# Attention and expert layers on one core: a planner's durations, the token ranks, the first denominators and the first loads are changed

## The chip, the core and the metric

The kernel runs on one core of a Trainium2 chip. The metric is the device time of one execution in microseconds (us). Engines are named as the profile names them: PE (TensorE) multiplies, DVE (VectorE) and ACT (ScalarE) do the element-wise work, POOL (GpSimd) casts and issues indirect DMAs, SP (SyncE) issues the other DMAs.

## What is computed

The reference has two parts. Attention over 8 batches, 12 heads, 448 tokens and 64 columns per head, with capped scores:

```
scores = cap * tanh(scale * (q @ k.T) / cap)        # cap = 30
attn   = exp(scores - max) / (sum + 1e-9)
x      = attn @ v                                   # heads side by side: 768 columns
```

and, batch by batch, one expert for the 128 tokens that score highest:

```
score   = x @ w_gate                                # 448 scores
top     = 128 tokens with the highest score
y       = relu(x[top] @ w1) @ w2                    # 768 -> 1024 -> 768
out     = x;  out[top] += sigmoid(score[top]) * y
```

## The kernel before, in words

**Doubles.** Four heads form a *double*: two row groups and two column groups of PE, 64 by 64 each, so that four matmuls (a *quartet*) run side by side. There are 24 doubles, three for each batch. A double has seven steps of 64 keys. A step is a quartet of scores on PE (L297, into `ps`), a tanh over 128x896 on ACT (L337), an exponential in place (L340, tile `p`), a quartet of products with v (L305, accumulated in `acc`), and on DVE an addition of the exponentials into `e` (L350, six per double). After the last step one quartet with a matrix of ones sums `e` over the keys (L384, `sums`), DVE transposes products (L376) and sums (L392), takes reciprocals (L398, L400), normalises (L425), and multiplies by the gate vector and reduces (L447, L451).

**Selection.** When a batch's three doubles are done, DVE adds the partial scores (L472, L474), PE folds them (L478) so that each token has its own partition, DVE copies them (L484), PE spreads them along a row (L489), DVE copies the row (L494) and counts for each token how many score higher (L502) and how many equal ones stand before it (L510), four pieces of 128 tokens each, adds the two counts (L517) and compares them with 0 to 127 (L553). PE multiplies that matrix with the token numbers and scores (L558), and POOL gathers the 128 rows from memory (L569).

**Expert.** The gathered rows and both weight matrices are split in a high and a low part, and three products of parts are summed, all in full 128x128 matmuls (L635): 36 of 512 columns for w1 and 48 of 384 for w2 in each batch. The text calls them *heavy*. The weights arrive in 14 pieces, through three staging buffers: SP loads a piece (L253), POOL casts it to the high part (L256), DVE subtracts to get the low part (L259).

**Order.** Every instruction of the fast path belongs to a task with an engine, an estimated duration, a priority, and buffers that it takes and gives back. `Plan.run` plays these tasks through by the estimates, before the kernel is built, and writes each engine's instructions in the order in which it started them. Engines work strictly in that order. `SEEN` is what the planner adds until another engine sees a result. On PE, `pick_pe` decides between attention (mode "att") and full-array work (mode "full"): it visits heavy work for `VISIT` = 2000 ns at a time, and while attention is left it stops heavy work when only `RESERVE` = 42000 ns of it remain. The reserve covers the last batch's selection.

Of the kernel before, what the change touches and what calls it, by code (L numbers as in the profile page):

```python
# [22 lines left out]
EPS = 1e-9  # L23
WARM = 3
# [3 lines left out]
SEEN = {"NONE": 0, "PE": 240, "ACT": 90, "DVE": 90, "POOL": 120, "SP": 0}  # L28
# [3 lines left out]
RESERVE = 42000  # L32


class Task:

    def __init__(self, eng, ns, fn, deps=(), prio=0.0, take=(), give=(), lat=0, mode=None,
                 heavy=False):
        self.eng, self.ns, self.fn, self.prio, self.lat = eng, ns, fn, prio, lat
        self.take, self.give, self.mode, self.heavy = take, give, mode, heavy  # L40
        self.after = []
# [7 lines left out]
class Plan:  # L49
# [28 lines left out]
    def run(self, after_attention):  # L78
# [4 lines left out]
        self.att_left = sum(t.mode == "att" for t in self.tasks)  # L83
        self.heavy_left = sum(t.ns for t in self.tasks if t.heavy)
# [4 lines left out]
        while started < len(self.tasks):  # L89
            for e in SEEN:  # L90
# [7 lines left out]
                if e == "PE":  # L98
# [4 lines left out]
                    if t.mode == "att":  # L103
                        self.att_left -= 1
                        if not self.att_left:
                            after_attention()
# [41 lines left out]
    def pick_pe(self):  # L148
# [22 lines left out]
def load_flag(tc, K, cap):  # L171
    nc = tc.nc
    cp = K.const
    K.cap = cp.tile([P, 1], F32, name="capc")
    nc.sync.dma_start(K.cap, cap.to_broadcast([P, 1]))
# [19 lines left out]
    K.rk = [cp.tile([P, K.NCH], F32, name=f"rk{i}") for i in range(2)]  # L195
    K.before = cp.tile([P, K.NCH * P], BF16, name="before")
    K.fold = cp.tile([P, 4, Q], F32, name="fold")
    K.ones = cp.tile([P, HD], F32, name="ones")
    K.hs = cp.tile([P, 1024], F32, name="hs")
    K.room = cp.tile([P, 6 * K.S], F32, name="room")  # L200
    K.used = 0

    def early(n):
        K.used += n
        return K.room[:, K.used - n:K.used]

    K.early = early


def load_consts(tc, K):  # L210
# [6 lines left out]
    for vt, sc, rk, far in zip(K.vals, K.score, K.rk, (1e6, 0.0)):  # L217
# [3 lines left out]
        nc.vector.memset(rk, far)  # L221
    nc.vector.tensor_reduce(K.fold[:, 0, :], K.ident.rearrange("p (a i) -> p i a", i=Q),
                            axis=AX.X, op=ALU.add)
    for g in range(1, 4):
        nc.vector.tensor_copy(K.fold[:, g, :], K.fold[:, 0, :])
    nc.gpsimd.memset(K.before, 1.0)
    nc.gpsimd.affine_select(K.before, K.before, pattern=[[-1, K.NCH * P]],
                            compare_op=ALU.is_gt, fill=0.0, base=(K.NCH - 1) * P,
# [85 lines left out]
def attention_tasks(tc, K, D):  # L314
# [13 lines left out]
    for s in range(NS):  # L328
# [18 lines left out]
        def sum2(t, s=s):  # L347
            if s == 1:
                D.E = w_tile(K, [P, 2, S], F32, "E", t.got["E"], "e")
# [558 lines left out]
```

## Time and profile before

| | |
|---|---|
| runs before | 496.62, 497.96, 499.25 us (median 497.96) |
| the profiled execution | 497.39 us, of which the profile's span is 495.7 us |
| first quartet, first heavy matmul, last four heavy matmuls begin | 6.60, 93.01, 488.52 us after the span's start |
| PE busy | 463.2 us (93% of the span) |
| DVE busy | 399.9 us (81%) |
| ACT busy | 346.8 us (70%) |
| POOL busy | 43.0 us (9%) |

The profile has one execution. A timeline row gives the start, the time from the first start to the last end, the engine, the instructions and, in brackets, how long the engine had been idle and what released it. Durations of neighbours overlap a little, so what an instruction costs its engine's queue is the distance between starts. A step's quartet on PE is eight records, since the profile shows each of the four float32 matmuls as two.

### The profile page before, as it was taken

The numbers are of one execution on the slowest core, as the hardware profiler recorded it, in microseconds if no ns is written. First come the engines' busy times: TensorE is split into PE (matmuls) and PEld (weight loads), VectorE is DVE, ScalarE is ACT, GpSimd is POOL, SyncE is SP. The second block draws the span as 40 slices with busy tenths as digits, with TensorE's granted clock in tenths as the row PEclk, the third lists the DMA queues.
The fourth block names the chain that finished last, engine by engine and source line by source line (L and its number), as shares of the span: only waits on it lengthen the run. The fifth ranks groups of instructions, "written<-read, shape, count | busy, mean of one in ns | idle before, by whom it ended". The sixth has DMA issues, their size and how long they took to land.

```text
span 495.7 us, 9354 instructions
## 1 busy us (share of the span) xinstructions
PE 463.2 (93%) x3750; PEld 243.3 (49%) x3750; DVE 399.9 (81%) x671; ACT 346.8 (70%) x394; POOL 43.0 (9%) x40
## 2 busy tenths in 40 slices
PE   5968999899999999999999999999999999859994
PEld 2222233443654465445554655455554533239984
DVE  1699999999989878988789679987789699987311
ACT  4957998679576986877777777977767799810210
POOL 1331121110020001100020000100020001000000
PEclk9988999999999999999999999999999999989998
DMA  6825864356141631553333532534323641032101
GB/s 212 337 85 177 204 191 132 113 141 173 56 153 47 180 96 39 176 128 96 112 103 105 158 75 74 176 95 130 112 70 119 176 112 34 0 75 70 33 32 38
DMA packets 50660, 57.42 MB, mean 116 GB/s; under 512 B 17968, under 2 KB 44720, under 8 KB 50608
## 3 DMA queue, kind: packets, MB, share of 16 engines
q1 hardware_dynamic: 49328, 50.44, 36.0%
q0 software_dynamic: 1280, 6.29, 3.8%
q8 instruction: 32, 0.52, 0.5%
q14 instruction: 20, 0.16, 0.1%
HBM read 42.57 MB, written 14.16 MB: 114 GB/s over the span
## 4 chain that ended last, share of the span: by engine, by line
PE 65%; DVE 19%; issue 5%; DMA 4%; ACT 4%; POOLq 0%; POOL 0%; DVEq 0%
PE pb L635 25%; PE acc L305 18%; PE ps L297 16%; DVE e L350 7%; PE sums L384 4%; ACT p L337 2%; PE pb L598 1%; DVE jk L447 1%; DMA xe<-out,idx 1%; DMA stage<-in_moe_w 1%; DVE part L451 1%; DVE sm L392 1%; ACT p L340 1%; DVE jk L502 1%; DMA q<-in_q 1%
## 5 line engine op out<-in xcount | busy, mean ns | idle before, releaser
L337 ACT ACTIVATE p<-ps,sc 128x896 f32<-128x896 f32 x168 | 165.0, 1007 | 84.7 <-PE ps L297 81.8
L340 ACT ACTIVATE p<-p,capc 128x896 f32<-128x896 f32 x168 | 170.4, 1046 | 2.0
L305 PE MATMUL acc<-p,v 64*64 64x448 f32 x1288 | 147.5, 552 | 2.0 <-ACT p L340 1.6
L297 PE MATMUL ps<-q,k 64*64 64x448 f32 x1288 | 145.4, 542 | 3.1 <-ACT p L337 1.8
L350 DVE TENSOR_TENSOR e<-e,p 128x896 f32<-128x896 f32 x120 | 132.1, 1101 | 20.0 <-ACT p L340 15.6
L297 PEld LDWEIGHTS ps<-q,k 64*64 64x64 f32 x1288 | 47.3, 133 | 80.5 <-issue 34.6
L305 PEld LDWEIGHTS acc<-p,v 64*64 64x64 f32 x1288 | 44.6, 134 | 71.8 <-issue 46.6
L569 POOL DMA_INDIRECT xe<-out,idx x8 | 13.1, 1634 | 297.8 <-DVE gt L575 297.8
L384 PE MATMUL sums<-e,ones 64*64 64x448 f32 x192 | 24.3, 577 | 12.1 <-DVE e L350 11.9
L376 DVE STREAM_TRANSPOSE xT<-acc 128x896 f32<-128x896 f32 x24 | 26.6, 1110 | 9.4 <-PE acc L305 9.3
L656 ACT ACTIVATE hs<-pb 128x512 f32<-128x512 f32 x16 | 9.5, 598 | 35.3 <-PE pb L635 34.6
L635 PE MATMUL pb<-w2l,hh 128*128 128x384 f32 x128 | 30.6, 349 | 0.0
L392 DVE STREAM_TRANSPOSE sm<-sums 128x896 f32<-128x896 f32 x24 | 26.6, 1107 | 4.8 <-PE sums L384 4.7
L350 DVE TENSOR_TENSOR e<-p 128x896 f32<-128x896 f32 x24 | 26.0, 1083 | 5.4 <-ACT p L340 5.4
L635 PE MATMUL pb<-w2h,hl 128*128 128x384 f32 x128 | 29.8, 346 | 0.0
L635 PE MATMUL pb<-w2h,hh 128*128 128x384 f32 x128 | 29.1, 350 | 0.5 <-DVE hl L605 0.5
L635 PE MATMUL pb<-w1h,xh 128*128 128x512 f32 x96 | 27.6, 409 | 0.0
L635 PE MATMUL pb<-w1h,xl 128*128 128x512 f32 x96 | 27.2, 405 | 0.0
L451 DVE TENSOR_REDUCE part<-jk 128x14 f32<-128x896 f32 x24 | 26.1, 1086 | 0.8
L635 PE MATMUL pb<-w1l,xh 128*128 128x512 f32 x96 | 26.1, 400 | 0.0
L635 PEld LDWEIGHTS pb<-w2h,hh 128*128 128x128 f32 x128 | 22.9, 192 | 5.1 <-issue 2.4
L635 PEld LDWEIGHTS pb<-w2h,hl 128*128 128x128 f32 x128 | 22.4, 189 | 2.8 <-issue 2.8
(82 smaller groups left out, 392.6 us busy)
## 6 DMA issues: line engine op xcount, KB each, us to landing
q<-in_q SPq DMA_DIRECT2D x46, 224.0 KB, 3.9
k<-in_k SPq DMA_DIRECT2D x46, 224.0 KB, 3.8
v<-in_v SPq DMA_DIRECT2D x23, 448.0 KB, 4.2
out<-xn SPq DMA_DIRECT2D x16, 224.0 KB, 4.4
out<-room SPq DMA_DIRECT2D x16, 224.0 KB, 3.7
stage<-in_moe_w SPq DMA_DIRECT2D x6, 384.0 KB, 3.0
stage<-in_moe_w SPq DMA_DIRECT2D x4, 512.0 KB, 6.9
out<-xn SPq DMA_DIRECT2D x16, 112.0 KB, 2.4
```

The source lines that it names most:

```text
L297: tc.nc.tensor.matmul(K.ps[HALF[r], j, :K.S], lhsT=D.k[r][HALF[j], ks], rhs=D.q[r][HALF[j], :], start=True, stop=True)
L305: tc.nc.tensor.matmul(D.acc[HALF[j], r, :K.S], lhsT=D.v[HALF[r], s, j, :], rhs=D.P[s][HALF[r], j, :], start=(s == 0), stop=(s == K.NS - 1))
L337: nc.scalar.activation(D.P[s], box["ps"][:, :, :S], AF.Tanh, scale=K.sc)
L340: nc.scalar.activation(D.P[s], D.P[s], AF.Exp, scale=K.cap)
L350: nc.vector.tensor_tensor(D.E, D.P[0] if s == 1 else D.E, D.P[s], op=ALU.add)
L376: nc.vector.transpose(D.xT, D.acc[:, :, :S])
L384: nc.tensor.matmul(D.sums[HALF[j], r, :S], lhsT=K.ones[HALF[r], :], rhs=D.E[HALF[r], j, :], start=True, stop=True)
L392: nc.vector.transpose(D.sm, D.sums[:, :, :S])
L451: nc.vector.tensor_reduce(K.part[b][:, grp, :], jk, axis=AX.X, op=ALU.add)
L569: nc.gpsimd.indirect_dma_start(out=X["xe"][:M], out_offset=None, in_=K.out[:(b + 1) * S, :], in_offset=bass.IndirectOffsetOnAxis(ap=X["idx ...
L635: nc.tensor.matmul(X["acc" + n_ops][:M, :ns[1]], lhsT=X[l][:, i, :M], rhs=K.wts[r][:, i, ns[2]], start=bool(start and n == 0), stop=(stop ...
L656: nc.scalar.activation(K.hs[:M, fs], X["acc" + nm][:M], AF.Relu)
```

## The change

- **Durations.** The planner's estimates become shorter: tanh and exponential 905 and 935 ns in place of 1030 and 1075, and others likewise; `SEEN` for ACT and DVE rises from 90 to 170.
- **Last sums.** The last double's sums are marked `late`; once only they are left of attention, heavy work is allowed below the reserve.
- **Ranks.** One operation for 128 tokens does both counts: it subtracts the token's own score from the row and compares with a table that holds a tiny positive number for the token itself and later ones, and zero for earlier ones (L536). The rank matrix is one operation (L569), the sum of two counts is gone, the fold is four matmuls of 32 columns so that two copies are enough (L513, L517, L520).
- **First two doubles.** DVE adds only the first five exponentials. The last two are summed on PE, by a quartet each, on top of the quartet for `e` (`sum_groups`, L416).
- **Loads.** The first q, k and v are issued before anything else, half of q and k and the cap on ACT's queue; the first three weight pieces are issued before the third double's q and k.

```
-SEEN = {..., "ACT": 90, "DVE": 90, ...}
+SEEN = {..., "ACT": 170, "DVE": 170, ...}
+EARLY = 2
...
-        if self.att_left and self.heavy_left <= RESERVE:
+        if self.main_left and self.heavy_left <= RESERVE:
             heavy = []
-        if self.mode == "att" and att:
+        if att and (self.mode == "att" or not self.main_left):
             return first(att)
...
+    tc.nc.scalar.dma_start(K.cap, cap.to_broadcast([P, 1]))
+    first.load_qk(tc, K, 0, None)
+    first.load_qk(tc, K, 1, None, tc.nc.scalar)
+    first.load_v(tc, K, None)
...
-        a = K.plan.add("SP", 600, load, prio=6 + 3 * n, ...)
+        a = K.plan.add("SP", 600, load, prio=6 + 3 * n if n > 2 else n - 4, ...)
-        l = K.plan.add("DVE", 1250, low, ...)
+        l = K.plan.add("DVE", 240 + 0.9 * m, low, ...)
...
+def sum_groups(d, n):
+    if d < EARLY:
+        return [list(range(n - 2)), [n - 2], [n - 1]]
+    return [list(range(n))]
...
-        th = add("ACT", 1030, tanh, ...)
-        ex_ = add("ACT", 1075, exp, ...)
+        th = add("ACT", 905, tanh, ...)
+        ex_ = add("ACT", 935, exp, ...)
...
+        for n, part in enumerate(parts):
             for r in range(2):
                 for j in range(2):
+                    nc.tensor.matmul(D.sums[HALF[j], r, :S], lhsT=K.ones[HALF[r], :],
+                                     rhs=part()[HALF[r], j, :], start=(n == 0),
+                                     stop=(n == len(parts) - 1))
+    su = add("PE", 752 * len(parts), sums, ready, ..., late=D.d == K.B * K.NG - 1)
...
-        nc.vector.tensor_scalar(jk[:m], box["row"][:m], score[:m, c:c + 1], None, op0=ALU.is_gt,
-                                op1=ALU.add, accum_out=rk[0][:m, c:c + 1])
...
+        nc.vector.scalar_tensor_tensor(out=jk[:m], in0=box["row"][:m], scalar=score[:m, c:c + 1],
+                                       in1=K.least[:m, at:at + S], op0=ALU.subtract,
+                                       op1=ALU.is_ge, accum_out=K.rk[:m, c:c + 1])
...
+        nc.vector.scalar_tensor_tensor(
+            out=X["sel"], in0=K.iota.unsqueeze(1).to_broadcast([P, NCH, P]), scalar=float(s0),
+            in1=K.rk.unsqueeze(2).to_broadcast([P, NCH, P]), op0=ALU.add, op1=ALU.is_equal)
```

What the planner makes of it, at three places. First DVE at the end of the first double (`w1l` is the low part of a weight piece, `stage` and `hs` are staging buffers). Before:

```order
L350 TENSOR_TENSOR e<-e,p 128x896 x2
L259 TENSOR_TENSOR w1l<-stage,w1h 128x1024
L350 TENSOR_TENSOR e<-e,p 128x896 x2
L259 TENSOR_TENSOR w1l<-stage,w1h 128x1024
L259 TENSOR_TENSOR w1l<-hs,w1h 128x1024
L350 TENSOR_TENSOR e<-e,p 128x896
L376 STREAM_TRANSPOSE xT<-acc 128x896
L392 STREAM_TRANSPOSE sm<-sums 128x896
```

With the change:

```order
L393 TENSOR_TENSOR e<-e,p 128x896 x2
L270 TENSOR_TENSOR w1l<-stage,w1h 128x1024 x2
L393 TENSOR_TENSOR e<-e,p 128x896
L270 TENSOR_TENSOR w1l<-hs,w1h 128x1024
L407 STREAM_TRANSPOSE xT<-acc 128x896
L270 TENSOR_TENSOR w1l<-stage,w1h 128x1024
L393 TENSOR_TENSOR e<-p 128x896
L427 STREAM_TRANSPOSE sm<-sums 128x896
```

The first double's last addition stood behind three weight pieces; its place is now behind two, and it is the fourth addition and not the sixth.

Second PE at the same place. Before:

```order
L305 MATMUL acc<-p,room 64x448 x4
L384 MATMUL sums<-e,ones 64x448 x4
L305 MATMUL acc<-p,v 64x448 x4
L297 MATMUL ps<-q,k 64x448 x4
```

With the change:

```order
L316 MATMUL acc<-p,room 64x448 x4
L416 MATMUL sums<-e,ones 64x448 x4
L416 MATMUL sums<-p,ones 64x448 x8
L316 MATMUL acc<-p,v 64x448 x8
L308 MATMUL ps<-q,k 64x448 x4
```

Two quartets are added behind the sums, and two products, not one, stand before the next scores.

Third PE where attention ends (23rd and 24th double). Before:

```order
L305 MATMUL acc<-p,v 64x448 x8
L384 MATMUL sums<-e,ones 64x448 x4
L297 MATMUL ps<-q,k 64x448 x4
L305 MATMUL acc<-p,v 64x448 x4
L297 MATMUL ps<-q,k 64x448 x4
L305 MATMUL acc<-p,v 64x448 x12
L384 MATMUL sums<-e,ones 64x448 x4
L635 MATMUL pb<-w2h,hh 128x384 x4
```

With the change:

```order
L653 MATMUL pb<-w1h,xh 128x512 x6
L653 MATMUL pb<-w1l,xh 128x512 x6
L653 MATMUL pb<-w1h,xl 128x512
L316 MATMUL acc<-p,v 64x448 x12
L308 MATMUL ps<-q,k 64x448 x4
L416 MATMUL sums<-e,ones 64x448 x4
L316 MATMUL acc<-p,v 64x448 x4
L308 MATMUL ps<-q,k 64x448 x4
L316 MATMUL acc<-p,v 64x448 x4
L308 MATMUL ps<-q,k 64x448 x8
L316 MATMUL acc<-p,v 64x448 x4
L653 MATMUL pb<-w1h,xl 128x512 x5
```

Before, the last 43 quartets of attention had no heavy matmul among them. Now heavy matmuls stand between them up to the last two steps, and as much heavy work as before is left behind the last sums. Over the whole program PE changes 114 times between the two kinds, before 106 times; ahead of the first heavy matmul stand 84 quartets of attention, before 80, and the four more are the added sums.

## Rows read from the trace of the kernel before

**Rows 1.** Busy time of each engine in four stretches (us; x is the number of records; PEclk is the granted clock as a share of full speed).

```profile
5.00:24.00 19.00, 18.19 (x142) 5.50 (x142) 9.04 (x19) 15.19 (x17) 5.70 (x7) 1.00 0.90 321
24.00:31.00 7.00, 1.92 (x12) 0.80 (x16) 6.03 (x6) 3.20 (x4) 3.02 (x2) 0.83 0.47 146
...
300.00:395.00 95.00, 94.76 (x782) 50.45 (x774) 80.15 (x135) 72.57 (x83) 5.08 (x4) 1.00 0.41 117
395.00:441.30 46.30, 38.17 (x361) 13.93 (x363) 44.52 (x77) 38.36 (x45) 1.83 (x1) 1.00 0.25 63
```

**Rows 2.** The timeline of the first 62 us, all engines: start, us, engine, instructions, idle time before and its releaser.

```profile
12.47 1.90 ACT L337 ACTIVATE p<-ps,sc 128x896 f32<-128x896 f32 x2
12.61 1.09 DVE L350 TENSOR_TENSOR e<-p 128x896 f32<-128x896 f32 x1 [5.44 <-ACT p L340]
...
15.33 2.29 DVE L350 TENSOR_TENSOR e<-e,p 128x896 f32<-128x896 f32 x2 [1.64 <-ACT p L340]
...
16.12 1.91 ACT L337 ACTIVATE p<-ps,sc 128x896 f32<-128x896 f32 x2
...
18.84 1.04 POOL L256 CAST w1h<-stage 128x1024 fp32r<-128x1024 f32 x1 [12.38 <-DMA stage<-in_moe_w]
...
19.92 1.23 DVE L259 TENSOR_TENSOR w1l<-stage,w1h 128x1024 fp32r<-128x1024 f32 x1 [2.29 <-POOL w1h L256]
...
20.13 1.92 POOL L256 CAST w1h<-stage 128x1024 fp32r<-128x1024 f32 x1 [0.24 <-DMA stage<-in_moe_w]
...
21.06 3.77 DVE L350 TENSOR_TENSOR e<-e,p 128x896 f32<-128x896 f32 x2
...
25.88 2.05 DVE L259 TENSOR_TENSOR w1l<-hs,w1h 128x1024 fp32r<-128x1024 f32 x1
...
29.08 1.77 PE L384 MATMUL sums<-e,ones 64*64 64x448 f32 x8 [5.43 <-DVE e L350]
...
30.93 1.12 DVE L392 STREAM_TRANSPOSE sm<-sums 128x896 f32<-128x896 f32 x1 [0.97 <-PE sums L384]
...
33.10 1.01 ACT L337 ACTIVATE p<-ps,sc 128x896 f32<-128x896 f32 x1 [5.90 <-PE ps L297]
...
44.70 0.98 PE L384 MATMUL sums<-e,ones 64*64 64x448 f32 x8 [1.96 <-DVE e L350]
```

**Rows 3.** The chain of work that ended last, first 100 us, in order of time: start, us, what.

```profile
12.26 6.54 DMA stage<-in_moe_w
...
84.25 6.92 DMA xe<-out,idx
...
93.01 4.67 PE pb L635 x19
```

**Rows 4.** The timeline of DVE around the first batch's selection, 45 to 95 us.

```profile
70.56 0.17 DVE L472 TENSOR_TENSOR score<-part 128x14 f32<-128x14 f32 x1
...
73.05 0.72 DVE L484 COPY score<-pb 32x4 f32<-32x4 f32 x4
...
76.46 0.68 DVE L502 TENSOR_SCALAR_CACHE_REDUCE jk<-row,score 128x448 bf16<-128x448 f32 x1
...
81.15 0.87 DVE L553 TENSOR_SCALAR sel<-iota,rank 128x128 fp32r<-128x128 f32 x4
81.94 1.08 DVE L350 TENSOR_TENSOR e<-e,p 128x896 f32<-128x896 f32 x1
82.94 0.95 DVE L259 TENSOR_TENSOR w2l<-hs,w2h 128x768 fp32r<-128x768 f32 x1
83.81 0.15 DVE L566 TENSOR_SCALAR idx<-pb 128x1 int32<-128x1 f32 x1
```

**Rows 5.** Groups of instructions with their shapes, whole span: busy us, mean ns of one, idle time before and its releaser.

```profile
L350 DVE TENSOR_TENSOR e<-e,p 128x896 f32<-128x896 f32 x120 | 132.1, 1101 | 20.0 <-ACT p L340 15.6
...
L510 DVE SCALAR_TENSOR_TENSOR jk<-row,score,before 64x448 bf16<-64x448 f32 x8 | 5.4, 674 | 0.0
...
L685 DVE SCALAR_TENSOR_TENSOR xe<-pb,gt,xe 128x384 f32<-128x384 f32 x16 | 9.8, 611 | 9.2 <-PE pb L635 9.2
```

**Rows 6.** The timeline of PE, 112 to 131 us, where attention and heavy matmuls alternate.

```profile
113.61 1.68 PE L297 MATMUL ps<-q,k 64*64 64x448 f32 x16
115.11 1.68 PE L305 MATMUL acc<-p,v 64*64 64x448 f32 x16
...
128.36 1.68 PE L297 MATMUL ps<-q,k 64*64 64x448 f32 x16
129.97 0.97 PE L635 MATMUL pb<-w2l,hh 128*128 128x384 f32 x4
```

**Rows 7.** The timeline of PE from 380 us to the end.

```profile
395.12 0.98 PE L305 MATMUL acc<-p,v 64*64 64x448 f32 x8
...
441.23 1.43 PE L384 MATMUL sums<-e,ones 64*64 64x448 f32 x8 [4.49 <-DVE e L350]
442.59 1.65 PE L635 MATMUL pb<-w2h,hh 128*128 128x384 f32 x4
...
445.89 0.86 PE L635 MATMUL pb<-w2h,hh 128*128 128x384 f32 x4
...
460.29 0.50 PE L558 MATMUL pb<-vals,sel 128*128 128x4 f32 x4
460.65 1.64 PE L635 MATMUL pb<-w1h,xl 128*128 128x512 f32 x6
```

More of the change, by code (lines that the diff above doesn't have):

```diff
@@ L23 @@
 EPS = 1e-9
+LEAST = 2.0 ** -120
 WARM = 3
@@ L26 @@
 QUAD = tuple(slice(Q * a, Q * a + Q) for a in range(4))
-SEEN = {"NONE": 0, "PE": 240, "ACT": 90, "DVE": 90, "POOL": 120, "SP": 0}
+SEEN = {"NONE": 0, "PE": 240, "ACT": 170, "DVE": 170, "POOL": 120, "SP": 0}
 SWITCH = {"att": 170, "full": 130}
@@ L83, in run @@
         self.att_left = sum(t.mode == "att" for t in self.tasks)
+        self.main_left = sum(t.mode == "att" and not t.late for t in self.tasks)
         self.heavy_left = sum(t.ns for t in self.tasks if t.heavy)
@@ L216, in load_consts @@
                    allow_small_or_imprecise_dtypes=True)
-    for vt, sc, rk, far in zip(K.vals, K.score, K.rk, (1e6, 0.0)):
+    for vt, sc in zip(K.vals, K.score):
         nc.vector.memset(vt.bitcast(F32), 0.0)
@@ L220, in load_consts @@
         nc.vector.memset(sc, 0.0)
[L221 to L228, printed above, removed]
+    nc.vector.memset(K.rk, 1e6)
+    nc.vector.tensor_reduce(K.fold, K.ident.rearrange("p (a i) -> p i a", i=Q), axis=AX.X,
+                            op=ALU.add)
+    nc.gpsimd.memset(K.least, 0.0)
+    nc.gpsimd.affine_select(K.least, K.least, pattern=[[-1, (K.NCH - 1) * P + K.S]],
+                            compare_op=ALU.is_gt, fill=LEAST, base=(K.NCH - 1) * P,
                             channel_multiplier=1)
 SIZES = {"qk": 2, "v": 3, "S": 2, "V": 1, "P": 7, "E": 2, "xT": 2, "sm": 1, "rec": 2, "xn": 2,
-         "bank": 2, "row": 1, "sel": 1, "rank": 2, "xe": 2, "xs": 1, "hsb": 1, "hx": 1,
+         "bank": 2, "row": 1, "sel": 1, "xe": 2, "xs": 1, "hsb": 1, "hx": 1,
          "stage": 3, "rk": 1}
@@ L260, in low @@
                                     op=ALU.subtract)
-        a = K.plan.add("SP", 600, load, prio=6 + 3 * n, take=("stage",), lat=5000)
+        a = K.plan.add("SP", 600, load, prio=6 + 3 * n if n > 2 else n - 4, take=("stage",), lat=5000)
         h = K.plan.add("POOL", 1300, high, [a], prio=n)
-        l = K.plan.add("DVE", 1250, low, [h], prio=6 + 3 * n, give=[("stage", a)])
+        l = K.plan.add("DVE", 240 + 0.9 * m, low, [h], prio=6 + 3 * n, give=[("stage", a)])
         K.weights[nm].append(l)
@@ L451, in scores @@
         nc.vector.tensor_reduce(K.part[b][:, grp, :], jk, axis=AX.X, op=ALU.add)
-    sc = add("DVE", 2160, scores, [n], prio=g0 + 2.5, take=("sm",))
+    sc = add("DVE", 2130, scores, [n], prio=g0 + 2.5, take=("sm",))
     sc.give = [("sm", sc)]
```

185 lines of the change are left out of this document (90 added, 95 removed).

## The prediction, made before the changed kernel ran

> **What bounds the kernel now.** I read the busy time by stretches first. From 300 to 395 us PE is busy 94.76 of 95 us: attention and heavy work alternate there and PE is the bound. From 395 to 441 us, where attention runs alone, PE is busy 38.17 of 46.3 us while DVE has 44.52: DVE and ACT set the pace [rows 1]. So what counts is PE's time as work plus loss: PE's work is fixed, and a gain must come from loss at the two ends.
>
> The start loses most. The first heavy matmul comes at 93.01 us, and until then PE has only 80 quartets of 0.75 us (two in 1.50 us [rows 6]), 60 us of work. Attention alone cannot fill PE: ACT needs 3.65 us for two steps (12.47 to 16.12 [rows 2]), PE 3.0 us. On top of that there are stalls. The timeline shows PE idle for 5.43 us before the first sums, released by the addition into `e`; ACT then waits 5.90 us for scores. The second sums wait 1.96 us in the same way [rows 2]. The chain of waits shows why the addition is late: it comes from a weight piece issued at 12.26 us that took 6.54 us to land [rows 3], after which DVE has three weight pieces between its additions. The granted clock is 0.83 over 24 to 31 us [rows 1], so the first sums also run partly at 1.2 GHz.
>
> The other end: the last sums wait 4.49 us for DVE, and the heavy matmuls behind them run slowly at first: from 441.23 to 445.89 us PE does one quartet and twelve matmuls [rows 7].
>
> **The sum, against the profiled execution's 497.4 us** (0.6 below the median, well inside the runs' spread).
>
> *1. The first heavy matmul comes earlier.* Its chain is DVE: additions and weight pieces from 12.61 us [rows 2] to the score totals at 70.56 us, the selection up to the index at 83.81 us [rows 4], then a gather of 6.92 us [rows 3].
> - To the totals the new order has 16 additions in place of 20: 4 x 1.10 us [rows 5] = -4.4 us. It has two more w2 pieces, 2 x 0.95 [rows 4] = +1.9.
> - Idle: 1.64 (second addition, stays), 2.29 and 0.97 us [rows 2]. By the order the first weight piece is issued after 11 loads on SP (three more are on ACT's queue) and not after 20, so the 2.29 goes; the transpose of the first products must still wait for the seventh exponential, about 1.6 us by ACT's 1.82 us per step. Idle 4.9 becomes 3.3: -1.6. Together -4.1 us at the totals.
> - From totals to index: counts, casts and rank sum took 76.46 to 81.15 = 4.69 us [rows 4]. The new operation is not in the trace. Its lower bound is the mean of one 384-element fused operation, 0.61 us; its upper bound is 0.67 us plus 0.08 for reading the accumulator. I take 0.60 between starts (the 448-element equality count is the nearest form, 0.674 with overlap [rows 5]). Four of them with 0.45 for casts and reads: 2.85, so -1.85. The rank matrix took 0.79 (81.15 to 81.94); one operation of 512 elements lies between 0.61 (384) and 1.10 (896) [rows 5]; taken 0.67: -0.1. Two copies for four: -0.37 of 0.72. The w2 piece ahead of the index goes to before the totals: -0.87 [rows 4]. Together -3.2.
>
> So the first heavy matmul moves by -7.3, to 85.7 us. Is attention as far by then? The order puts the same steps ahead of it, and ACT's 35 steps after the first two end 35 x 1.82 us after 12.47 [rows 2], at 76 us plus waits; the 5.90 us wait shrinks to about 1 (three quartets of sums and two products, 3.7 us, while ACT still has an exponential pair), so yes. The four added quartets, 3.0 us of PE work, lie in this stretch where PE waits anyway: nothing. If that cover is gone they cost 3.0. Bounds of this part: -3 (only the additions count, and the w2 pieces eat half) to -10.4 (the idle time goes as well).
>
> *2. The end.* From 395.12 to 445.89 us [rows 7], 50.8 us, PE does 43 + 1 quartets (33.0 us), some 20 small matmuls (1.6) and twelve heavy ones (2.1): 36.7 of work, 14 us lost. In the new order heavy matmuls stand among these quartets until two steps before the end, and they are not extra work. What stays lost: a change between the two kinds costs about 0.11 us (128.36 to 129.97 is 1.61 against 1.50 [rows 6]), some 20 changes, 2.2 us; the last two steps' tanh and exponential pass ACT one after the other, about 2; the last sums wait for one addition, about 0.5. So 4.7 in place of 14: -9.3. Bounds: -4 (the last sums still wait as long and the slow clock stays) to -12.
>
> *3. Work added on PE's bound stretch.* Eight changes more, +0.9. The fold becomes eight records of at most 4 columns for two; four records of 4 columns took 460.29 to 460.65 = 0.36 [rows 7], so 0.72 at most for the eight; lower bound nothing. I take +0.2 for each of 8 batches, +1.6; bounds 0 to +4.
>
> *4. At nothing.* The rest of the DVE time saved by the ranks, about 2.4 us for each later batch, lies beside heavy work (PE 94.76 of 95 us). The last batch's chain is hidden: its selection ends at 460.29, with heavy work to the end. The q and k on ACT's queue: the first scores follow the cap's flag, which still takes one load. Longer table and memset on POOL: POOL is idle there.
>
> Sum: 497.4 - 7.3 - 9.3 + 0.9 + 1.6 = 483.3; I say **483 us**.
>
> **Rivals.**
> - *Slower: the tight plan stalls PE at each change.* The estimates for a step fall from 2.105 to 1.84 us, against 1.82 measured; nothing is spare. If at each of the some 50 returns to attention the first product waits for its exponential, PE loses 50 times that wait. Against: before, ACT and DVE had 76% and 84% of the stretch from 300 to 395 us [rows 1], and the new order gives DVE less and ACT no more beside the same work of PE. It decides from 0.28 us a time, where the gain of 14 is gone; at 0.4 it gives 483 + 20 = 503. Chance 0.05.
> - *The first stage gains little: casts and additions collide.* POOL's cast took 1.04 us while DVE stood still (18.84) and 1.92 beside additions (20.13); two additions then took 3.77 us and a weight piece 2.05 [rows 2]. Ten casts, not eight, now lie ahead of the totals. My sum keeps the stretching of before, about 5 us (58 less 4.9 of idle time and some 48 of operations at their usual distance). If each of the ten held DVE for a cast's 1.04 us it would be 10.4, so 5.4 of the 7.3 are lost: 489. Chance 0.12. The Trainium skill (SBUF — State Buffer, section SBUF: two separate sides) says that a DVE operation with two SBUF inputs and a POOL operation hold a shared port pair exclusively, and that the loser blocks entirely; that would make each collision cost a whole operation. The rows agree in direction, and by the full rule the time would be this rival's.
> - *The end stays DVE's.* The last addition comes late again and the clock falls with it; only half of part 2: 488. Chance 0.08.
> - *The change doesn't do what it says:* the weights are issued earlier but land no earlier, because 5 to 24 us are full (DMA share 0.90 [rows 1]). Then the 2.29 us idle stays and more with it; with the additions saved but the end as forecast, about 487. Chance 0.06.
>
> **Numbers.** The forecast has 0.69, with a range of its own of 477 to 488. The rivals at 487 to 489 hold most of the upper rest; the slower one lies beyond. Low end: both ends at their lower bounds, 497.4 - 10.4 - 12 = 475. High end: part 1 at -3, part 2 at -4, part 3 at +0.5: 491. Range 475 to 491. What a measurement can tell from no change is 0.5%, 2.5 us: faster 0.92, same 0.03, slower 0.05.
>
> **What would show it.** Right: PE's wait before the first sums gone (below 1 us), ACT's first long wait about 1 us; totals near 66.5 and first heavy matmul near 85.7 us; DVE's selection from row copy to rank matrix near 3 us; heavy matmuls between quartets up to some 10 us before the last sums, whose wait is under 1.5 us. Wrong: the first heavy matmul after 90 us, new waits of quartets for ACT or DVE in the middle that add up to over 5 us, or a last wait of over 4 us.

## The result and the profile after

The changed kernel takes **485.02 us** (median of 4 runs, 484.76 to 486.12) against 497.98 us before (496.62 to 499.25): a ratio of 0.9744, 95% interval 0.9715 to 0.9774. The profiled execution took 484.88 us, its span is 483.0. The forecast was 483 us with a range of 475 to 491.

The stages first: busy time of each engine (PE, PEld, DVE, ACT, POOL; x is the number of records), then granted clock, DMA share, GB/s, in the changed kernel.

```profile
5.00:24.00 19.00, 18.10 (x138) 5.75 (x142) 10.66 (x18) 14.38 (x17) 6.72 (x7) 1.00 0.91 331
24.00:31.00 7.00, 6.16 (x68) 2.27 (x64) 6.40 (x7) 4.87 (x6) 3.93 (x3) 1.00 0.67 208
300.00:395.00 95.00, 94.83 (x803) 48.63 (x800) 76.24 (x107) 75.19 (x85) 4.71 (x3) 1.00 0.44 122
395.00:430.00 35.00, 33.73 (x286) 14.86 (x284) 29.68 (x44) 28.11 (x33) 1.83 (x1) 1.00 0.18 47
```

Set beside [rows 1], two stages have changed. From 24 to 31 us PE is busy 6.16 us where it was 1.92, at a granted clock of 1.00 for 0.83. And in the last attention stage PE is busy 33.73 of 35 us, where it was 38.17 of 46.3; DVE, which had 44.52 of those 46.3, now has 29.68 of 35 and is no longer the bound. From 300 to 395 us PE looks as full as before. That is misleading, as will be seen.

The granted clock of the whole execution is 1.000, before 0.987. Before, it was 0.50 (1.2 GHz) in three stretches of 3.4 us, from 28.6, 45.7 and 441.6 us on, each beside one of the waits of the sums ([rows 2], [rows 7]); the changed kernel has none until its last matmul has ended. Three times 3.4 us at half the clock is at most some 5 us of PE's work, an estimate of what the clock has in the gains at the two ends.

The first stage in the timeline of the changed kernel, PE and ACT (start, us, instructions, idle time before and its releaser):

```profile
25.61 0.98 PE L416 MATMUL sums<-e,ones 64*64 64x448 f32 x8 [0.84 <-ACT p L354]
26.41 1.68 PE L416 MATMUL sums<-p,ones 64*64 64x448 f32 x16
...
56.76 0.98 PE L416 MATMUL sums<-e,ones 64*64 64x448 f32 x8 [1.64 <-DVE e L393]
...
86.05 1.65 PE L653 MATMUL pb<-w1h,xh 128*128 128x512 f32 x6
```

```profile
30.45 1.01 ACT L354 ACTIVATE p<-ps,sc 128x896 f32<-128x896 f32 x1 [2.13 <-PE ps L308]
...
43.66 1.01 ACT L354 ACTIVATE p<-ps,sc 128x896 f32<-128x896 f32 x1 [1.85 <-PE ps L308]
```

PE's wait of 5.43 us before the first sums is 0.84, ACT's 5.90 us is 2.13 [rows 2]. The third sums now wait, 1.64 us. The first heavy matmul is at 86.05 us (93.01 before, [rows 3]).

The first batch's selection on DVE in the changed kernel:

```profile
65.91 0.17 DVE L506 TENSOR_TENSOR score<-part 128x14 f32<-128x14 f32 x1
...
70.63 0.59 DVE L530 COPY row<-pb 128x448 f32<-128x448 f32 x1
71.25 0.69 DVE L536 SCALAR_TENSOR_TENSOR jk<-row,score,least 128x448 bf16<-128x448 f32 x1
71.86 0.08 DVE L536 DVE_READ_ACCUMULATOR jk<-row,score,least 128x1 f32 x1
71.98 0.69 DVE L536 SCALAR_TENSOR_TENSOR jk<-row,score,least 128x448 bf16<-128x448 f32 x1
...
74.33 0.68 DVE L569 SCALAR_TENSOR_TENSOR sel<-iota,rk 128x512 fp32r<-128x512 f32 x1
74.93 1.08 DVE L393 TENSOR_TENSOR e<-e,p 128x896 f32<-128x896 f32 x1
75.93 0.15 DVE L584 TENSOR_SCALAR idx<-pb 128x1 int32<-128x1 f32 x1
```

Against [rows 4]: totals 70.56 to 65.91, index 83.81 to 75.93. Counts and matrix take 71.25 to 74.93, 3.68 us, where they took 76.46 to 81.94, 5.48 us.

The end, PE in the changed kernel:

```profile
427.47 0.98 PE L316 MATMUL acc<-p,v 64*64 64x448 f32 x8 [0.45 <-ACT p L357]
429.27 0.98 PE L316 MATMUL acc<-p,v 64*64 64x448 f32 x8 [0.81 <-ACT p L357]
...
430.49 0.59 PE L653 MATMUL pb<-w2h,hh 128*128 128x384 f32 x2
431.00 0.98 PE L416 MATMUL sums<-e,ones 64*64 64x448 f32 x8
431.92 0.62 PE L653 MATMUL pb<-w2h,hh 128*128 128x384 f32 x2
```

The last sums wait for nothing (4.49 us in [rows 7]) and the heavy matmuls behind them run at full speed at once.

**Loss by stretch.** To compare kernels I took PE's timeline apart: each row's distance to the next start, less its work (0.75 us a quartet [rows 6], 0.234 us for a heavy record of 512 columns, 0.174 for one of 384, 0.09 for a small one, all read from undisturbed stretches). What is left is loss: waits, changes between the kinds of work, slow clock. "Start" runs to the first heavy matmul, "end" is the stretch of the last 44 quartets, "middle" lies between, "tail" is what follows. Where the kernel has the four added quartets of sums, their 3.0 us are counted in the start's loss, so that the rows add up; the expectations of c1 and c2 count it without them. The sums agree with the measured differences within about 1.5 us, and a single cell is no better than 1 to 2 us: counted record by record with one price for each kind, the middle of the kernel before comes out above 20 us, and what the change loses there is nearer 4 us than the 5.1 of the table. The column "heavy at the end" counts the heavy matmuls that stand among the last 44 quartets. The last column is from the waits of PE's weight loads in the middle: how long those of products waited for their exponential. Such a wait lies mostly beside a running matmul, so it is not itself loss.

| kernel | us | start | middle | end | tail | heavy at the end | products' loads wait for exp |
|---|---|---|---|---|---|---|---|
| before | 497.98 | 26.0 | 19.1 | 13.6 | 2.0 | 3 | 6.4 |
| changed | 485.02 | 17.6 | 24.2 | 5.0 | 1.1 | 50 | 26.0 |
| a1_loads_on_sp | 484.88 | 18.7 | 24.2 | 5.1 | 1.1 | 50 | 26.4 |
| a2_no_early | 492.68 | 24.6 | 25.3 | 5.3 | 1.1 | 50 | 27.0 |
| a3_weights_late | 483.84 | 19.6 | 23.0 | 4.1 | 1.4 | 65 | 29.5 |
| a4_old_durations | 492.64 | 25.7 | 18.8 | 10.0 | 1.0 | 15 | 4.8 |
| b1_plan_only | 496.14 | 28.4 | 22.9 | 8.0 | 1.1 | 46 | 26.3 |
| b2_ranks_only | 488.57 | 24.5 | 16.5 | 8.5 | 1.1 | 41 | 5.6 |
| b3_act_1980 | 487.72 | 23.1 | 19.3 | 7.2 | 1.2 | 32 | 6.3 |
| b4_late_1980 | 484.87 | 22.5 | 17.0 | 7.7 | 1.1 | 36 | 5.3 |
| c1_middle_1980 | 480.42 | 17.8 | 19.0 | 6.2 | 1.3 | 48 | 7.5 |
| c2_middle_late | 482.72 | 20.3 | 18.5 | 6.7 | 1.1 | 47 | 6.9 |
| c3_no_early_late | 492.66 | 24.4 | 23.8 | 5.8 | 1.1 | 50 | 25.0 |
| c4_old_late | 493.00 | 23.6 | 19.8 | 10.0 | 1.0 | 15 | 4.9 |

By this table the change won 8.4 us at the start and 9.5 at end and tail, and lost 5.1 in the middle. The start's loss is counted from the first quartet, which came 0.85 us later than before (7.45 for 6.60); the first heavy matmul itself moved by 6.96 us.

### The profile page after: what moved, and what is told of

The parts are those of the page before. It is cut to its first block, busy times and chain, and to the rows that moved or that the text cites. A ratio compares the mean times of both kernels' runs of the same rounds, so it can differ in the third digit from the quotient of the medians.

```text
span 483.0 us, 9396 instructions
## 1 busy us (share of the span) xinstructions
PE 466.7 (97%) x3830; PEld 238.3 (49%) x3830; DVE 377.0 (78%) x551; ACT 348.6 (72%) x394; POOL 45.1 (9%) x40
## 4 chain that ended last, share of the span: by engine, by line
PE 75%; DVE 10%; issue 5%; ACT 4%; DMA 3%; SPq 0%; POOLq 0%; POOL 0%; DVEq 0%; ACTq 0%
PE pb L653 25%; PE acc L316 22%; PE ps L308 20%; PE sums L416 3%; DVE e L393 3%; PE pb L616 2%; DMA stage<-in_moe_w 2%; ACT p L354 2%; ACT p L357 1%; DVE w1l L270 1%; DVE jk L482 1%; PE pb L576 1%; PE pb L525 1%; DVE xn L460 1%; DVE part L486 1%
## 5 line engine op out<-in xcount | busy, mean ns | idle before, releaser
L393 DVE TENSOR_TENSOR e<-e,p 128x896 f32<-128x896 f32 x116 | 126.3, 1089 | 38.7 <-ACT p L357 33.8
L316 PE MATMUL acc<-p,v 64*64 64x448 f32 x1288 | 152.3, 550 | 1.9 <-ACT p L357 1.5
L308 PE MATMUL ps<-q,k 64*64 64x448 f32 x1288 | 143.9, 540 | 0.0
L316 PEld LDWEIGHTS acc<-p,v 64*64 64x64 f32 x1288 | 40.6, 132 | 82.5 <-ACT p L357 45.1
L653 PE MATMUL pb<-w2l,hh 128*128 128x384 f32 x128 | 28.7, 339 | 0.0
L653 PE MATMUL pb<-w2h,hl 128*128 128x384 f32 x128 | 28.2, 337 | 0.0
L653 PE MATMUL pb<-w1l,xh 128*128 128x512 f32 x96 | 27.5, 405 | 0.0
L653 PE MATMUL pb<-w1h,xh 128*128 128x512 f32 x96 | 27.1, 409 | 0.0
L712 POOL DMA_INDIRECT out<-xe,idx x8 | 10.2, 1277 | 166.4 <-DVE xe L703 116.1
L416 PE MATMUL sums<-e,ones 64*64 64x448 f32 x192 | 23.0, 550 | 2.7 <-DVE e L393 1.6
L653 PEld LDWEIGHTS pb<-w2h,hh 128*128 128x128 f32 x128 | 21.5, 188 | 7.3 <-issue 4.9
```

Of the source, the lines that this page charges most:

```text
L308: tc.nc.tensor.matmul(K.ps[HALF[r], j, :K.S], lhsT=D.k[r][HALF[j], ks], rhs=D.q[r][HALF[j], :], start=True, stop=True)
L316: tc.nc.tensor.matmul(D.acc[HALF[j], r, :K.S], lhsT=D.v[HALF[r], s, j, :], rhs=D.P[s][HALF[r], j, :], start=(s == 0), stop=(s == K.NS - 1))
L393: nc.vector.tensor_tensor(box["E"], box["E"] if n else D.P[s0], D.P[s], op=ALU.add)
L416: nc.tensor.matmul(D.sums[HALF[j], r, :S], lhsT=K.ones[HALF[r], :], rhs=part()[HALF[r], j, :], start=(n == 0), stop=(n == len(parts) - 1))
L653: nc.tensor.matmul(X["acc" + n_ops][:M, :ns[1]], lhsT=X[l][:, i, :M], rhs=K.wts[r][:, i, ns[2]], start=bool(start and n == 0), stop=(stop ...
L712: nc.gpsimd.indirect_dma_start(out=K.out[:(b + 1) * S, :], out_offset=bass.IndirectOffsetOnAxis(ap=X["idx"][:M, :1], axis=0), in_=X["xe"][ ...
```

## The experiments

### One part undone

**a1_loads_on_sp.** All first loads on SP's queue, the cap first.

```
-    tc.nc.scalar.dma_start(K.cap, ...)
+    tc.nc.sync.dma_start(K.cap, ...)
-    first.load_qk(tc, K, 1, None, tc.nc.scalar)
+    first.load_qk(tc, K, 1, None)
```

> The change, with the first loads back on SP's queue, the cap first (all else as changed; the planner's order is the same). Theory: the cap on ACT's queue landed at 4.70 us and not at 3.85, and everything waits for the flag made of it; so the first quartet comes at about 6.6 in place of 7.45 and the time falls by 0.8, to 484.2. Rival: the first q and k arrive earlier on two queues, and taking that back costs 0.3 to 1 us, 485.3 to 486.

Measured 484.88 us, ratio to before 0.9744 (0.9720 to 0.9769): the changed kernel's time, between the theory's 484.2 and the rival's 485.3, and too near to both to choose. The first quartet does come earlier, 6.50 for 7.45 us, and the exponentials by 1.06. DVE in this kernel shows where that goes:

```profile
24.27 1.10 DVE L407 STREAM_TRANSPOSE xT<-acc 128x896 f32<-128x896 f32 x1
26.93 1.22 DVE L270 TENSOR_TENSOR w1l<-stage,w1h 128x1024 fp32r<-128x1024 f32 x1 [1.55 <-POOL w1h L267]
```

DVE stands 1.55 us for the cast of a weight piece, 0.53 in the changed kernel; totals (65.99) and first heavy matmul (86.12) stay. The queue of the first loads is worth nothing either way.

**a2_no_early.** The sums of the first two doubles by DVE again, and so four quartets fewer.

```
-EARLY = 2
+EARLY = 0
```

> The change without the sums of single exponentials on PE (EARLY = 0): four more additions on DVE, 4.4 us, four quartets less on PE, 3.0 us, all before the first heavy matmul. Theory (DVE's chain sets the first heavy matmul, PE has room there): first heavy matmul 3 to 4.4 us later, at 89 to 90.5, time 488 to 489. Rival (the weights ahead alone do it, and DVE has slack): first heavy matmul unchanged, time 485, or 483 to 482 with the four quartets gone.

Measured 492.68 us (0.9902, 0.9872 to 0.9933), 7.7 over the changed kernel, well over what I expected. The first heavy matmul is only 3.4 us later, 89.43, but 76 quartets stand ahead of it and not 80 (without the added ones): attention is 3.0 us of PE work behind as well. The time of the first heavy matmul alone does not measure the start; the loss up to it does: 24.6 for 17.6.

**a3_weights_late.** The first three weight pieces back at their old place among the loads.

```
-        a = K.plan.add("SP", 600, load, prio=6 + 3 * n if n > 2 else n - 4, ...)
+        a = K.plan.add("SP", 600, load, prio=6 + 3 * n, ...)
```

> The change with the first three weight pieces issued at their old priority. Theory: DVE waits again for the first piece, about 2 us, and the first heavy matmul comes 2 to 3 us later, near 88.5; time 487 to 488. Rival (DVE's sum of work, not the pieces' arrival, sets the first heavy matmul): within 1 us of 485.

Measured 483.84 us (0.9725, 0.9692 to 0.9757): the rival's side, if anything faster. The start loses 2.0 us more, middle, end and tail together 1.8 less. "Weights ahead" buys nothing here.

**a4_old_durations.** The planner's old numbers in the changed kernel.

```
-SEEN = {..., "ACT": 170, "DVE": 170, ...}
+SEEN = {..., "ACT": 90, "DVE": 90, ...}
-        th = add("ACT", 905, ...)
-        ex_ = add("ACT", 935, ...)
+        th = add("ACT", 1030, ...)
+        ex_ = add("ACT", 1075, ...)
...
```

> The change with the planner's old durations and its old SEEN for all tasks that both kernels have. The order then has no heavy matmuls among the last 35 quartets or so, as before. Theory: first heavy matmul near 86 to 87; the middle loses less in waits of products for exponentials (5 us less than the change), the end loses 8 to 10 us more: time 488 to 490. Rival (the tight durations only harm): the middle's gain is as large as the end's loss or larger, time 484 or below.

Measured 492.64 us (0.9906, 0.9874 to 0.9938), 7.6 over the changed kernel. The rival fell, and the theory's 488 to 490 was passed as well. The middle loses 5.4 **less**, as the theory had it, and the end 5.0 more where it had 8 to 10. What it did not have is the start: 8.1 more, with the first heavy matmul at 91.29 us and not at 86 to 87. DVE in this kernel:

```profile
13.06 1.09 DVE L393 TENSOR_TENSOR e<-p 128x896 f32<-128x896 f32 x1 [5.03 <-ACT p L357]
16.98 1.23 DVE L270 TENSOR_TENSOR w1l<-stage,w1h 128x1024 fp32r<-128x1024 f32 x1 [2.82 <-POOL w1h L267]
18.12 2.93 DVE L393 TENSOR_TENSOR e<-e,p 128x896 f32<-128x896 f32 x2
```

and in the changed kernel:

```profile
13.73 1.09 DVE L393 TENSOR_TENSOR e<-p 128x896 f32<-128x896 f32 x1 [5.57 <-ACT p L357]
16.45 2.36 DVE L393 TENSOR_TENSOR e<-e,p 128x896 f32<-128x896 f32 x2 [1.63 <-ACT p L357]
18.73 4.03 DVE L270 TENSOR_TENSOR w1l<-stage,w1h 128x1024 fp32r<-128x1024 f32 x2
```

With slower exponentials in the plan, the weight piece is thought to be ready before the second addition and is put ahead of it. On the chip the cast is late and DVE stands 2.82 us with ready additions behind.

### One part alone, and two

**b1_plan_only.** The kernel before with the change's durations, `SEEN` and the rule for the last sums.

```
-        th = add("ACT", 1030, ...)
-        ex_ = add("ACT", 1075, ...)
+        th = add("ACT", 905, ...)
+        ex_ = add("ACT", 935, ...)
... (the other durations, SEEN and late= as in the change)
```

> The kernel before with the change's planning alone: its durations of operations, its delay until a result is seen, and the rule that lets the last sums stand behind heavy work. No addition, count, load or weight is moved by hand. Taking the old durations back out of the changed kernel cost 7.6 us, most of it at the start (first heavy matmul 5.2 us later, 3 quartets fewer ahead of it). Theory: that gain is made with DVE's room, the additions that the sums by matmuls take off DVE; here DVE has all 20 additions ahead of the first totals, and the order leaves the last 45 quartets without heavy work as before. So little: first heavy matmul within 2 us of 93.0, first sums still wait more than 3 us, 495 to 498. Rival: the durations alone set the order of weight pieces and additions, and the gain comes by itself: first heavy matmul at 88 to 90, 490 to 492.

Measured 496.14 us (0.9976, 0.9960 to 0.9993): the theory's time, but not by its details. The first heavy matmul is 2.9 us later (95.92), the first sums wait 1.45 us and not over 3. The end gains 5.6 us, against what I expected; start and middle give it back (+2.4, +3.8).

**b2_ranks_only.** The kernel before with the change's selection, nothing else.

```
+        nc.vector.scalar_tensor_tensor(out=jk[:m], in0=box["row"][:m], scalar=score[:m, c:c + 1],
+                                       in1=K.least[:m, at:at + S], op0=ALU.subtract,
+                                       op1=ALU.is_ge, accum_out=K.rk[:m, c:c + 1])
... (fold, copies and rank matrix as in the change; loads, sums and durations as before)
```

> The kernel before with the change's selection alone: ranks in one operation per 128 tokens, rank matrix in one operation, two copies for four, eight small fold matmuls. Theory: from the totals to the index 13.25 us in the kernel before, 10.02 in the changed one, of the difference 0.87 is a weight piece, so about 2.4 us less here (10.0 to 11.0 us from totals to index); the order puts 77 quartets ahead of the first heavy matmul and not 80, which takes 2.25 us of it back. So 495 to 498, first heavy matmul at 90 to 91.5. Rival: the room on DVE, 2.4 us in each of 8 batches, also shortens the middle and the end, and it is 491 to 494.

Measured 488.57 us (0.9845, 0.9818 to 0.9873): both missed, since even the rival had 491 at best, though its direction is right. The theory's own two numbers nearly hold (totals to index 70.23 to 80.23, 10.0 us; first heavy matmul 89.73, just under its 90), but most of the gain is elsewhere: 1.5 us at the start, 2.6 in the middle, 5.1 at the end. PE at this kernel's end:

```profile
429.89 1.92 PE L316 MATMUL acc<-p,v 64*64 64x448 f32 x16 [1.74 <-ACT p L357]
433.44 0.98 PE L416 MATMUL sums<-e,ones 64*64 64x448 f32 x8 [1.63 <-DVE e L393]
434.35 0.96 PE L653 MATMUL pb<-w2h,hh 128*128 128x384 f32 x4
```

The last sums wait 1.63 us for DVE, 4.49 before [rows 7]. DVE's busy time over the span falls from 399.9 to 381.6 us, 2.3 for each batch, and in 395 to 430 us from 33.82 to 28.89: the stage in which DVE was the bound. The two rows, before and in b2:

```profile
395.00:430.00 35.00, 33.31 (x317) 12.72 (x320) 33.82 (x66) 34.05 (x41) 1.83 (x1) 1.00 0.22 58
```

```profile
395.00:430.00 35.00, 32.24 (x296) 14.05 (x292) 28.89 (x42) 29.82 (x36) 0.97 (x1) 1.00 0.24 65
```

The room on DVE is not the only thing that has changed there. The planner makes another order of the shorter selection: 41 heavy matmuls stand among the last 44 quartets, before 3. No run gives DVE the room at a fixed order, so the two are not told apart.

**c3_no_early_late** and **c4_old_late** fill a table: selection in both, sums by matmuls yes or no, durations old or new, the weights at their old place in all.

```
c3, to the changed kernel:            c4, to a4_old_durations:
-EARLY = 2                            -  prio=6 + 3 * n if n > 2 else n - 4
+EARLY = 0                            +  prio=6 + 3 * n
-  prio=6 + 3 * n if n > 2 else n - 4
+  prio=6 + 3 * n
```

> The kernel before with the change's selection and its planning durations, without the sums by matmuls in the first two groups and without the early weights. With the selection alone it was 488.57, with everything but the sums by matmuls 492.68, with everything but the durations 492.64. Theory: durations and sums by matmuls pay only together; one without the other is worth nothing beside the selection, since the tight plan needs the room that the sums by matmuls leave on DVE at the start. So 488 to 492. Rival: each is worth something by itself and the early weights cost it in the two kernels named: 485.5 to 487.5.

> The changed kernel with the planner's old durations and with the first weight loads at their old place. With the old durations and early weights (492.64) all six pieces of w1 stood on DVE ahead of its second addition, and DVE waited 2.8 us for a cast. Theory: that loss is the early weights', so here it goes and the sums by matmuls are worth what they save on DVE: 486 to 488, first heavy matmul at 87.5 to 89.5. Rival: with the old durations the sums by matmuls cost PE work without giving an earlier start: 490 to 493, first heavy matmul after 90.

| us (start's loss) | old durations | new durations |
|---|---|---|
| sums by DVE | 488.57 (24.5), b2 | 492.66 (24.4), c3 |
| first sums by matmuls | 493.00 (23.6), c4 | 483.84 (19.6), a3 |

c3 came out slightly above its theory's 488 to 492 (0.9901, 0.9879 to 0.9923), c4 at its rival's upper end (0.9905, 0.9881 to 0.9929; its first heavy matmul at 89.10, as the theory had it). Each part alone, on top of the selection, makes the kernel 4 us **slower**; together they make it 5 us faster. (a3, c3 and c4 also have the `late` mark and the first loads on ACT's queue, b2 has neither. The queue is worth nothing in the changed kernel by a1; `late` was not tried alone.)

The stages say where. Against b2, c3 loses 7.3 more in the middle and 2.7 less at the end, with the same start. a3 loses 6.5 more in the middle and 4.4 less at the end, and 4.9 less at the start. So the new durations cost the middle with or without the added sums (the next section shows how) and help the end; what the two parts do only together is at the start. There, in c3, the tight plan brings PE too early to the gathered rows:

```profile
79.52 0.61 PE L576 MATMUL pb<-vals,sel 128*128 128x4 f32 x4
86.59 1.54 PE L616 MATMUL pb<-ident,xe 128*128 128x128 f32 x6 [6.46 <-DMA xe<-out,idx]
```

PE stands 6.46 us, since the index came late on DVE (81.28) and nothing else stands ahead of these transposes; the granted clock is 0.50 (1.2 GHz) from 84.3 to 91.2 us. b2 has a wait of 5.57 us before its first sums, with the clock at 0.50 from 27.1 to 33.9 us. In a3 no wait of PE between its first quartet and its first heavy matmul is above 2.3 us and the clock stays at 1.00. That is not the whole either, since c4 has no longer waits (1.9 us) and the full clock, and its start is only 0.9 better than that of b2. In c4 the totals come 1.35 us earlier than in b2 (68.88 for 70.23) and the index 0.54 (79.69 for 80.23), while the added quartets cost PE 3.0; middle and end lose 3.3 and 1.5 more. At its end 15 heavy matmuls stand among the last 44 quartets, in b2 41. Why the planner's order comes out so, and why the middle loses, I have not settled.

### The middle

PE's weight loads that waited for ACT in the middle (us in all, times, longest), in the changed kernel, in b2_ranks_only and in c1_middle_1980:

```profile
PEld acc L316 <- ACT p L357: 26.0, 39, 0.9
```

```profile
PEld acc L316 <- ACT p L357: 5.6, 17, 0.9
```

```profile
PEld acc L316 <- ACT p L357: 7.5, 19, 0.9
```

All kernels with 905 and 935 in the middle's plan have 25 to 30 us of this wait, all with more have 4.8 to 7.5 (last column of the table). ACT in the changed kernel shows why 905 and 935 are short there:

```profile
206.39 1.89 ACT L354 ACTIVATE p<-ps,sc 128x896 f32<-128x896 f32 x2
208.17 1.97 ACT L357 ACTIVATE p<-p,capc 128x896 f32<-128x896 f32 x2
211.56 1.01 ACT L354 ACTIVATE p<-ps,sc 128x896 f32<-128x896 f32 x1 [1.42 <-PE ps L308]
212.60 1.04 ACT L357 ACTIVATE p<-p,capc 128x896 f32<-128x896 f32 x1
213.55 0.99 ACT L354 ACTIVATE p<-ps,sc 128x896 f32<-128x896 f32 x1
214.57 1.05 ACT L357 ACTIVATE p<-p,capc 128x896 f32<-128x896 f32 x1
```

Where PE is the bound, tanh and exponential of one step mostly alternate singly (72 tanhs alone and 19 pairs from 86 to 380 us), and a step then takes 1.99 us (211.56 to 213.55); at the start, in pairs, 1.82 (13.60 to 17.24 us for two). The plan has 1.84. So it puts products right behind scores more often, and too early: from start to start they lose 4.6 us at 65 places of the changed kernel's middle, and some 0.6 at 37 places both before and in c1_middle_1980.

**b3_act_1980.** Durations as they are when single, everywhere.

```
-        th = add("ACT", 905, ...)
-        ex_ = add("ACT", 935, ...)
+        th = add("ACT", 960, ...)
+        ex_ = add("ACT", 1020, ...)
```

> The changed kernel with the plan's two ACT durations at 960 and 1020 ns in place of 905 and 935: what a step's tanh and exponential take on ACT where they alternate singly (1.98 us), in place of what they take in pairs (1.82). Theory: in the changed kernel the products wait for their exponential at some 74 places between 86 and 381 us, 4.6 us in all, because the plan counts 1.84 us for a step. With 1.98 planned that wait falls below 1.5 us and the stretch loses some 20 us in place of 24.2; the end loses up to 2 us more, since the order leaves the last 26 quartets without heavy work. 481 to 484. Rival: the waits of products come from something the durations don't set (the order on ACT's queue, or PE coming early by its own lead), and the middle's loss stays at 23 to 25: 484.5 to 487.

Measured 487.72 us (0.9813, 0.9792 to 0.9833): slower than the changed kernel, and above the rival's range. Yet the middle did what the theory says (19.3, wait 6.3), and the end (2.2 more). The start was not in it: 23.1 for 17.6, a weight piece ahead of the second addition as in a4 (at 17.02, after 1.51 us for the cast), third sums waiting 3.14 us for DVE.

**b4_late_1980.** The same, with the weights at their old place.

```
b3's edit, and
-        a = K.plan.add("SP", 600, load, prio=6 + 3 * n if n > 2 else n - 4, ...)
+        a = K.plan.add("SP", 600, load, prio=6 + 3 * n, ...)
```

> The changed kernel with both: ACT's durations 960 and 1020 in the plan, and the first weight loads at their old place in the order (which by itself gave 483.84 for 485.02). Theory: the two add up, since one is about the middle and the other about what stands ahead of the first heavy matmul: 480 to 483. Rival: the gain of the late weights was that its order leaves fewer returns to attention in the middle, which the longer ACT durations also give, so it comes only once: 483 to 485.

Measured 484.87 us (0.9760, 0.9737 to 0.9783): the rival's range, but not for the rival's reason; the middle is as low as 17.0, and the start (22.5) and end (7.7) take it back.

**c1_middle_1980.** Long durations in the middle alone.

```
+        th = add("ACT", 960 if 6 <= D.d < 21 else 905, ...)
+        ex_ = add("ACT", 1020 if 6 <= D.d < 21 else 935, ...)
```

> The changed kernel with the plan's two ACT durations at 960 and 1020 ns for the attention steps of the 7th to the 21st group of heads alone; the first six and the last three groups keep the change's 905 and 935. With the long durations everywhere the time was 487.72: the middle lost 19.3 us and not 24.2, the waits of products for ACT were gone, but the first heavy matmul came 4.2 us later and the end lost 2.2 more. Theory: the two durations act in separate stretches, the short ones where ACT runs in pairs (start and end), the long ones where PE is the bound. So first heavy matmul at 86.0 with 84 quartets ahead, start loss 14 to 15, middle 19 to 21, end 5 to 6.5: 480 to 482. Rival: what the middle saves is given back, since the order is another one from the 7th group on and the heavy work left for the end differs: 483.5 to 486.

Measured **480.42 us** (480.17 to 481.77; 0.9657, 0.9633 to 0.9681): the theory, and faster than the changed kernel, whose interval begins at 0.9715. Start 17.8 (14.8 as the expectation counts it), middle 19.0, end 6.2. The stages:

```profile
24.00:31.00 7.00, 6.16 (x68) 2.50 (x68) 6.58 (x8) 4.84 (x7) 3.84 (x4) 1.00 0.65 198
300.00:395.00 95.00, 94.63 (x791) 49.61 (x783) 77.28 (x110) 74.49 (x86) 5.65 (x4) 1.00 0.45 128
```

PE's busy time from 300 to 395 us does not tell this kernel from the changed one (94.63 against 94.83). Over the span, PE is busy 460.5 us here and 466.7 there for the same instructions (3830 records): matmuls that wait for their weights' data seem to be shown as busy. That would be why the full stretch of the first table hid the loss.

**c2_middle_late.** c1 with the weights at their old place.

```
c1's edit, and
-        a = K.plan.add("SP", 600, load, prio=6 + 3 * n if n > 2 else n - 4, ...)
+        a = K.plan.add("SP", 600, load, prio=6 + 3 * n, ...)
```

> As before, with the long ACT durations in the middle alone, and the first weight loads at their old place in the order as well (by itself 483.84). Theory: the start is that of the late weights (first heavy matmul near 88, 85 quartets ahead of it, start loss 16 to 17), the middle 17 to 20, the end 5 to 7: 479.5 to 482. Rival: late weights and longer durations again give their gain only once, as with the durations long everywhere (484.87): 483 to 485.

Measured 482.72 us (0.9710, 0.9680 to 0.9741), above the theory's range and below the rival's. The middle has its 18.5, but the start has 20.3 (17.3 as the expectation counts it, with the first heavy matmul at 89.35 and not near 88). So beside the long durations in the middle the early weights are worth 2.5 us at the start; the changed kernel loses its 2.0 again later, c1 keeps them.

## Why the prediction was right, step by step

The time was 2 us above the forecast: the two large terms were right in size, one loss was missed, one small term was not there, and a saving was put at nothing that has a part in the end. That the sum came so near is in part luck, since the missed loss and the term that was not there partly cancel.

1. **The start** was to bring the first heavy matmul forward by 7.3 us; it came 6.96 earlier. Its chain: totals at 65.91 (forecast 66.5), though the first addition came 1.12 us later (13.73 for 12.61), which the prediction did not have; DVE's idle time up to the totals, 2.2 us where 3.3 were forecast (1.63 and 0.53), made up for it. Totals to index 10.02 us where it was 13.25, just the 3.2 less. Within this the counts took 0.73 us from start to start and not 0.60: 0.61 to the read, and the next one 0.12 behind that. Counts and matrix are 3.68 us where the steps say 3.52. The wait before the first sums fell as foreseen (0.84), ACT's long wait to 2.13 and not 1. From index to first heavy matmul it takes 10.12 us, 9.20 before. The step that attributes the gain to fewer additions was too simple: c4 has the fewer additions and the shorter selection, and its start is only 2.4 better than before. What made them count were the new durations (19.6 in a3). The rows of a4 show one way, a weight piece that is late put ahead of ready additions; that it is the whole is not shown.
2. **The end** was to give 9.3; end and tail gave 9.5, and by the mechanism of the step: 50 heavy matmuls stand among the last 44 quartets, where 3 stood. Over all kernels the end's loss goes roughly with that count (3: 13.6, 15: 10.0, 41: 8.5, 46: 8.0, 50: 5.0 to 5.8). Two parts of the change make such an order: the durations by themselves take 5.6 us off the end (b1, 46), the ranks 5.1 (b2, 41), both 7.8 (c3) to 8.6. At nearly the same count the end still loses 8.0 without the new ranks (b1) and 5.8 with them (c3); so some 2 us may be their room on DVE, which no run shows alone.
3. **Work in the bound stretch.** The changes between the kinds of work were to cost 0.9 more. The middle lost 5.1 by the table, and this is the step that failed: it priced the switches and not that products would come before their exponentials (4.6 us, before some 0.6). The prediction's own sign of being wrong, new waits of over 5 us in the middle, stayed about 1 us short of that. The fold's 1.6 is not there. PE in the changed kernel:

```profile
66.41 0.24 PE L513 MATMUL pb<-score,fold 128*32 128x4 f32 x8
66.59 1.76 PE L316 MATMUL acc<-p,v 64*64 64x448 f32 x16
```

   Eight records in 0.18 us, the lower bound. By the table the misses are 4.2 in the middle, less 1.6 here and 1.3 at the two ends (8.4 and 9.5 against 7.3 and 9.3): 1.3 us, of the 1.6 between the sum (483.3) and the profiled execution (484.88). The table itself is no better than 1.5 us, so this shows no more than that nothing large is missing.
4. **At nothing.** The rest of the time that the ranks save on DVE was said to lie beside heavy work. b2 shows that wrong: the shorter selection is worth 7.7 us in the middle and at the end, with the order that the planner makes of it. The row that spoke against it was in the prediction itself, DVE with 44.52 of 46.3 us in the last attention stage [rows 1]; a saving on the engine that bounds a stage is not free cover. The loads on ACT's queue were at nothing, and are (a1).

**The rivals.** *The tight plan stalls PE at each return to attention*: this is what happens in the middle, far below the point from which it decides. Products right behind scores lost 4.6 us over 65 places in the changed kernel, 0.07 us each, against the 0.28 at which the gain would be gone. *Casts and additions collide* would have given 489; totals came earlier than in the sum, though 13 casts and not ten began ahead of them, and though the collision is there: two weight pieces took 4.03 us beside two casts (18.73, above). The Trainium skill (SBUF — State Buffer, section SBUF: two separate sides) has the loser of the shared port blocked entirely. The two pieces are some 1.7 us longer than two of 1.15, near the 2.1 us of two casts, so this row leans to the rule; the sum of the start does not need it. *The end stays DVE's* fell (last sums without a wait). *The change doesn't do what it says*: the first cast did begin earlier, at 15.63 for 18.84 us, and it is worth nothing in the changed kernel (a3).

**Open.** Several of these numbers are those of one order each. A part's price depends on which others are there (the table of four), and c2 against c1, or c3's single wait of 6.46 us, show that 2 to 6 us can hang on where one instruction stands. Of the 19 us that the best kernel still loses in its middle about half may be changes between the kinds of work: PE changes there 87 times, as in the changed kernel, and at the 0.11 us of [rows 6] that is 9.6 us, an estimate that no run tests.

## What to carry to other kernels

A planner's durations should be those of the stage in which the work runs: the same step took 1.82 us in pairs and 1.99 singly, and planning with each in its own stage was 4.6 and 7.3 us faster than with either of them everywhere. Price a part of a change in the stage where its engine is the bound, and ask for each saving on DVE or ACT which stage that is. Undo parts and add parts: here one part undone cost 7.6 us, the same part alone gained 1.3, and on top of another part it cost 4. With a planner each such run has another order as well as other work, so count what the order did before a gain is put down to an engine's room.

## What was not expected of the hardware

- A tanh followed by the exponential of the same tile costs ACT 0.17 us a step more than two tanhs followed by two exponentials (1.99 and 1.82 us, 128x896).
- A fused operation with a count at its end takes 0.67 us for 448 elements, of 128 tokens or of 64 (means), and 0.73 from start to start with its read.
- Eight matmul records with 32 columns of weights and at most 4 columns of data took 0.18 us, the two of 14 columns before 0.14 to 0.32 from start to the next start, in the median 0.24.
- PE's busy time differs, 466.7 and 460.5 us, for the same records in two kernels of which one waits more for the data of its weight loads: a full PE row is not yet a PE at work.
